# Whole tiles for VectorE's product and row sums, and half of one projection block in lanes 0 to 63

## The chip, the core and the metric

The kernel runs on one core of one Trainium2 chip. The metric is the device time of one launch in microseconds (us); 663.65 us is the median of three runs of the kernel before (663.64 to 663.78). A core has four compute engines here: TensorE (PE in the profile; PEld is its weight loads), VectorE (DVE), ScalarE (ACT) and GpSimd (POOL). SyncE (SP) issues nearly all transfers. Sixteen DMA engines move the data between device memory (HBM) and the on-chip memory SBUF, which has 128 partitions, called lanes below. TensorE writes its sums into PSUM.

## The reference

One decoding step of a transformer layer with two parallel branches, for a batch of four rows `x` of 640 numbers, in bf16:

```
xn  = layernorm(x)
q   = xn @ wq                                  # 32 heads of 128
s   = einsum('bhqd,bhkd->bhqk', q, k_cache) * 128 ** -0.5
o   = einsum('bhqk,bhkd->bhqd', softmax(s), v_cache)
A   = concat_heads(o) @ wo                     # 4096 x 640
B   = gated MLP of xn (gelu, layernorm, w_in, w_out)
out = x + A + B
```

The two caches hold 4 batches x 32 heads x 4096 positions x 128 numbers each. Every number of them is read once: 128 MB of keys and as much of values, out of 282 MB that the kernel moves. `wo` is 5 MB.

## The kernel before

**Tiles.** The 32 heads are worked through in 8 groups of 4 (`HG`, `HT`), and each group in 4 batch rows, which gives 32 turns, i = 4 * group + batch row. Turn i has one tile of keys and one of values, each 128 lanes x 16384 bf16 (4 MB): a lane holds 128 positions (`NC`) of one head, so that lanes 0 to 31 hold the first head of the group, and so on. Five SBUF slots (`KV_SLOTS`) take keys and values in rotation. `pump` (L140) issues the next loads of the list `loads` as soon as the tile five places earlier is marked as used; all of them go through the one queue of SP, in order. The keys of the last turns are loaded early (`EXTRA_K`), so that the last tile to arrive is one of values, cut in four (`V_CUTS`).

**A turn.** The order of instructions on PE, DVE, ACT and SP is written out by hand (L672 to L740). For the keys of turn i:

- `product` (L457, DVE) multiplies the tile in place by the query, one call for each half of the tile (`HC` = 64 positions).
- `fold_half` (L466, DVE) adds the upper 64 of 128 numbers onto the lower, a half tile a call.
- `sums` (L475, PE) adds eight slices of the folded half up in PSUM, with an identity as weights, into `s_ps`; 8 numbers are left for each position.
- `row_sums` (L486, DVE) adds those 8 up, a half a call.
- `lane_max` (L495, DVE), `lay_max` (L501, ACT), `spread_max` (L508, PE) and `head_max` (L515, DVE) find the largest score of a head; `exps` (L524, ACT) exponentiates, and L533 (POOL) lays the result out as `pm`, the weights for the values.

These last steps are done for turn i - 1 inside turn i. `blocks` (L548, PE, 32 matmuls) multiplies a tile of values by its `pm`; after each second tile ACT copies the result (L558), and `gather` (L569, PE) sorts it by head. In the turns before the end the values lag one turn behind the keys, later two and three. In the last turn the blocks of turns 28 and 29 are both done, and after the loop those of 30 and 31.

**A group's end.** `group_den` (POOL L593, PE L600, DVE L602) adds up the exponentials, `group_norm` (L607, DVE) divides, `group_turn` (L616, PE) and `group_pick` (L627, L635, DVE) move four rows of the projection's input into every lane, and `group_proj` (L647, PE) multiplies by the group's block of `wo` (128 lanes x 4 rows x 640, 640 KB, one transfer, L159). Only the last group's block is laid out by head and comes in four transfers (L157). The blocks of the groups 6 and 7 are issued behind the last values, and their projections are the last matmuls of the kernel; ACT and DVE then copy the sums (L737, L738), and two small transfers store them.

The order of one turn before:

```
product(i, 0); row_sums(i-1, 1); maxima of i-1; group_pick and group_proj of an earlier group
fold_half(i, 0); head_max(i-1); exps(i-1); sums(i, 0); product(i, 1)
blocks(j), group_den; row_sums(i, 0); fold_half(i, 1); gather(j), group_norm
sums(i, 1); group_turn; pump()
```

Of the kernel before, what the change touches and what calls it, by code (L numbers as in the profile page):

```python
# [9 lines left out]
FP32 = mybir.dt.float32  # L10
BF16 = mybir.dt.bfloat16
ACT = mybir.ActivationFunctionType
ALU = mybir.AluOpType
AX = mybir.AxisListType
# [7 lines left out]
def kernel(  # L22
# [14 lines left out]
    nc = tc.nc  # L37
    P = nc.NUM_PARTITIONS
    Bsz, Sq, D = A_x.shape
    _, H, S, Dh = A_k_cache.shape  # L40
# [4 lines left out]
    scale_qk = float(Dh) ** -0.5  # L45
# [3 lines left out]
    HT = 4  # L49
    HG = H // HT  # L50
    NT = HG * Bsz
    LN = P // HT
    NC = HT * S // P
    HC = NC // 2
    HD2 = Dh // 2
    RW = 8
# [4 lines left out]
    NOH = D // 2  # L61
# [8 lines left out]
    const = ctx.enter_context(tc.tile_pool(name="const", bufs=1))  # L70
    work = ctx.enter_context(tc.tile_pool(name="work", bufs=1))
    small = ctx.enter_context(tc.tile_pool(name="small", bufs=2))
    PSUM = bass.MemoryType.PSUM
    ps_s = ctx.enter_context(tc.tile_pool(name="ps_s", bufs=2, space=PSUM))
    ps_pv = ctx.enter_context(tc.tile_pool(name="ps_pv", bufs=2, space=PSUM))
    ps_m = ctx.enter_context(tc.tile_pool(name="ps_m", bufs=2, space=PSUM))
    ps_out = ctx.enter_context(tc.tile_pool(name="ps_out", bufs=1, space=PSUM))
# [12 lines left out]
    for c0, c1 in ((0, HT), (HT, DC)):  # L90
        t = slot("wq")[:, 0 : (c1 - c0) * HD].rearrange("p (c n) -> p c n", n=HD)
# [58 lines left out]
    wo_h = A_wo.rearrange("(j h p) n -> j p h n", p=P, h=HT)  # L150
    wo_tiles = {}

    def load_wo(j):
        wo_tiles[j] = wop.tile([P, HT, D], BF16, name="wo")
        if j == HG - 1:
            for hh in range(HT):
                nc.sync.dma_start(out=wo_tiles[j][:, hh, :], in_=wo_h[j][:, hh, :])  # L157
            return
        nc.sync.dma_start(out=wo_tiles[j][:].rearrange("p r n -> p (r n)"), in_=wo_r[j])  # L159

# [10 lines left out]
    eps_tile = const.tile([P, 1], FP32)  # L171
    nc.vector.memset(eps_tile[:], eps)
    head_scale = const.tile([P, P], FP32)
    nc.vector.memset(head_scale[:], 0.0)
    lane_diag = const.tile([P, LN], FP32)
    nc.vector.tensor_reduce(
        out=lane_diag[:],
# [1 line left out]
        axis=AX.X,  # L179
        op=ALU.add,  # L180
    )
    for hh in range(HT):
        ps = slice(hh * LN, (hh + 1) * LN)
        nc.vector.memset(head_scale[ps, ps], scale_qk)
    ones_sq = const.tile([P, P], FP32)
    nc.vector.memset(ones_sq[:], 1.0)

# [10 lines left out]
            op=ALU.add,  # L198
        )

    hmask = const.tile([P, HT], FP32)
    nc.vector.memset(hmask[:], 0.0)
    for hh in range(HT):
        nc.vector.memset(hmask[hh * LN : (hh + 1) * LN, hh : hh + 1], 1.0)
    spread = const.tile([P, HT, HT, LN], BF16)
    nc.vector.tensor_copy(
        out=spread[:],
# [2 lines left out]
        ),  # L210
    )


    q_lanes = const.tile([HT * Bsz, Bsz, P], BF16)
    nc.vector.tensor_copy(
# [84 lines left out]
    def out_sum(half):  # L300
        return out_ps[OG * half : OG * half + Bsz, :]
# [132 lines left out]
    def stage_q(hg):  # L434
        g, ps = hg % CG, slice(hg % CG * LN, (hg % CG + 1) * LN)
        qr_ps = ps_m.tile([HT * Bsz, Dh], FP32, tag="m", name="qr_ps")
        for hh in range(HT):
            nc.tensor.matmul(
                out=qr_ps[:],
                lhsT=place[ps, hh, :],  # L440
                rhs=q_sb[ps, hg // CG, hh * Dh : (hh + 1) * Dh],
                start=(hh == 0),
                stop=(hh == HT - 1),
            )
        q_rows = small.tile([HT * Bsz, Dh], BF16, name="q_rows")
        nc.scalar.copy(out=q_rows[:], in_=qr_ps[:])
        qb_ps = ps_m.tile([P, Bsz, Dh], FP32, tag="m", name="qbc_ps")
        for b in range(Bsz):
            nc.tensor.matmul(
                out=qb_ps[:, b, :], lhsT=q_lanes[:, b, :], rhs=q_rows[:], start=True, stop=True  # L450
            )
        qbcs[hg] = small.tile([P, Bsz, Dh], BF16, name="qbc")
        nc.scalar.copy(out=qbcs[hg][:], in_=qb_ps[:])

    def product(i, half):
        t = k_tiles[i][:, half * HC : (half + 1) * HC, :]
        nc.vector.tensor_tensor(  # L457
            out=t,
            in0=t,
            in1=qbcs[i // Bsz][:, i % Bsz, None, :].to_broadcast([P, HC, Dh]),  # L460
            op=ALU.mult,
        )

    def fold_half(i, half):
        t = k_tiles[i][:, half * HC : (half + 1) * HC, :]
        nc.vector.tensor_tensor(  # L466
            out=t[:, :, 0:HD2], in0=t[:, :, 0:HD2], in1=t[:, :, HD2:Dh], op=ALU.add
        )

    def sums(i, half):  # L470
        t = k_tiles[i][:, half * HC : (half + 1) * HC, :]
        s = sums_ps[i, half] = ps_s.tile([P, HC, RW], FP32, name="s_ps")
        n = HD2 // RW
        for g in range(n):
            nc.tensor.matmul(  # L475
                out=s[:],
                lhsT=ident[:],
                rhs=t[:, :, g * RW : (g + 1) * RW],
                start=(g == 0),
                stop=(g == n - 1),  # L480
            )

    def row_sums(i, half):
        if half == 0:
            scores[i] = small.tile([P, NC], FP32, name="s_sb")
        nc.vector.tensor_reduce(  # L486
            out=scores[i][:, half * HC : (half + 1) * HC],
            in_=sums_ps.pop((i, half))[:],
            axis=AX.X,
            op=ALU.add,  # L490
        )

    def lane_max(i):
# [67 lines left out]
    def gather(i, stop=True):  # L561
        if i % 2 == 0:
            return
        hg, b = divmod(i, Bsz)
        if b == 1:
            pvs[hg] = ps_pv.tile([P, HT, Bsz], FP32, tag="pv", name="pv")
        pv_sb = blocks_sb.pop(i)
        for k in range(GC):
            nc.tensor.matmul(  # L569
                out=pvs[hg][:, :, b - 1 : b + 1],  # L570
                lhsT=pv_sb[:, k * Dh : (k + 1) * Dh],
                rhs=sel[:, k, :, :],
                start=(k == 0),
                stop=stop and k == GC - 1,
            )
# [67 lines left out]
    def group_proj(hg):  # L643
        o_n = gr.pop(hg)
        for hh in range(HT):
            for half in range(2):
# [5 lines left out]
                    stop=(hg == HG - 1 and hh == HT - 1),  # L652
                )

    def group(i, fn):
        if 0 <= i < NT and i % Bsz == Bsz - 1:
            fn(i // Bsz)

    def at(i, fn, *args):
        if 0 <= i < NT:  # L660
            fn(i, *args)
# [10 lines left out]
    with tc.manual_schedule(engines={E.PE, E.DVE, E.Activation, E.SP}):  # L672
        stage_q(0)
        gmlp()
        used.update(occupants[:3])
        pump()
        for i in range(NT):
            j = turns.get(i)
            product(i, 0)
            at(i - 1, row_sums, 1)  # L680
            at(i - 1, lane_max)
            at(i - 1, lay_max)
            at(i - 1, spread_max)
            group(turns.get(i - 1, -1), group_pick)
            if turns.get(i - 1, -1) // Bsz < HG - 2:
                group(turns.get(i - 1, -1), group_proj)
            fold_half(i, 0)
            at(i - 1, head_max)
            at(i - 1, exps)
            sums(i, 0)  # L690
            product(i, 1)
            if i % Bsz == 2 and i // Bsz + 1 < HG:
                stage_q(i // Bsz + 1)
            due = [] if j is None else [j]
            if i == NT - 1:
                due += range(j + 1, NT - 2)
            for n, jj in enumerate(due):
                if n:
                    gather(due[n - 1])
                blocks(jj)  # L700
                group(jj, group_den)
                used.add(("v", jj))
            row_sums(i, 0)
            fold_half(i, 1)
            if due:
                gather(due[-1])
            for jj in due:
                group(jj, group_norm)
            sums(i, 1)
            for jj in due:  # L710
                group(jj, group_turn)
            used.add(("k", i))
            pump()
            if i % Bsz == 2 and i // Bsz < HG - 2:
                load_wo(i // Bsz)
        load_wo(HG - 2)
        load_wo(HG - 1)
        row_sums(NT - 1, 1)
        lane_max(NT - 1)
        lay_max(NT - 1)  # L720
        spread_max(NT - 1)
        head_max(NT - 1)
        exps(NT - 1)
        blocks(NT - 2)
        group_den(HG - 1)
        blocks(NT - 1, 0, V_CUTS[1])
        gather(NT - 1, stop=False)
        for c0, c1 in zip(V_CUTS[1:], V_CUTS[2:]):
            pairs(NT - 1, c0, c1)
        group_norm(HG - 1)  # L730
        group_proj(HG - 2)
        group_proj(HG - 1)

        res = work.tile([P, NOH], BF16, name="res")
        out_v = out.flatten_outer_dims()
        r0, r1 = slice(0, Bsz), slice(OG, OG + Bsz)
        nc.scalar.copy(out=res[r0], in_=out_ps[r0])  # L737
        nc.vector.tensor_copy(out=res[r1], in_=out_ps[r1])  # L738
        nc.scalar.dma_start(out=out_v[:, 0:NOH], in_=res[r0])
        nc.sync.dma_start(out=out_v[:, NOH:D], in_=res[r1])  # L740
# [30 lines left out]
```

## Time and profile before

| what | value |
|---|---|
| median of three runs | 663.65 us (663.64 to 663.78) |
| span of the profiled execution, first to last instruction | 661.6 us |
| what lies around the span (median less span) | 2.05 us |
| moved from and to HBM | 282.24 MB read, 0.01 MB written, 427 GB/s over the span |
| DVE busy | 491.5 us, 74% |
| PE busy | 348.7 us, 53%, at a mean granted clock of 0.726 |
| POOL busy | 151.3 us, 23% |
| ACT busy | 49.3 us, 7% |

The page gives no time for the profiled execution other than its span, so the sums below are made against the span. Each engine's share of busy time is a mean over the whole span. The row of DMA digits in the page's second part is the mean busy share of the sixteen DMA engines in each fortieth of the span. In the answers of the trace a line of the timeline has the start, the busy time, the engine, the kernel's line and the operation, and in brackets the idle time before it with what ended that. In a table by windows the columns are the busy time of each engine (with the number of instructions), the granted TensorE clock, the share of the DMA engines that was busy and GB/s.

### The profile page before, as it was taken

The page shows a single profiled execution, that of the slowest core. Times are in us where ns is not written, and L with a number is a line of the kernel's source. Part 1 is how long each engine was busy: PE and PEld are TensorE (multiplying, and loading weights), DVE is VectorE, ACT ScalarE, POOL GpSimd, SP SyncE. Part 2 cuts the span into 40 slices and gives each one's busy share as a digit, 9 for nine tenths or more (in the row PEclk, how much of TensorE's full clock was granted, in tenths as well). Part 3 has the DMA queues.
Part 4 walks back from the last instruction along what each step waited for, and adds up shares of the span by engine and source line. Part 5 has one row for each costly group of instructions (what it writes and reads, how often), then busy time and mean ns, then how long its engine had stood idle before and what let it go on. Part 6 is the DMA issues. An engine that isn't in the chain of part 4 may idle for free.

```text
span 661.6 us, 5115 instructions
## 1 busy us (share of the span) xinstructions
PE 348.7 (53%) x2109; PEld 144.6 (22%) x2109; DVE 491.5 (74%) x334; ACT 49.3 (7%) x138; POOL 151.3 (23%) x57
## 2 busy tenths in 40 slices
PE   2526653646445455663745654465643756435567
PEld 1402211212121121221212222121211312112124
DVE  2299797867789677788776698776787899777950
ACT  0201100001000010001000000000100000000010
POOL 3002222112222112222112222112222133122230
PEclk9999676776767777766678657777576577688585
DMA  9999999999999999999999999999999999999997
GB/s 368 432 438 429 430 440 427 440 423 434 442 416 447 424 433 442 423 440 424 433 440 423 440 428 431 442 421 442 422 435 442 422 441 428 427 442 428 429 428 289
DMA packets 11971, 282.57 MB, mean 427 GB/s; under 512 B 1344, under 2 KB 1964, under 8 KB 3244
## 3 DMA queue, kind: packets, MB, share of 16 engines
q1 hardware_dynamic: 11928, 282.25, 99.2%
q8 instruction: 16, 0.26, 0.1%
q14 instruction: 7, 0.06, 0.0%
q10 hardware_dynamic: 20, 0.01, 0.0%
HBM read 282.24 MB, written 0.01 MB: 427 GB/s over the span
## 4 chain that ended last, share of the span: by engine, by line
issue 49%; DMA 25%; POOL 15%; DVE 7%; PE 3%; SPq 1%; ACT 0%; POOLq 0%; DVEq 0%; ACTq 0%
DMA k_nat<-in_A_k_cache_dram 20%; POOL pm L533 15%; DMA wo<-in_A_wo_dram 4%; DVE k_nat L457 4%; DVE k_nat L466 2%; PE s_ps L475 2%; PE pv_acc L548 1%; SPq L123 0%; DVE s_sb L486 0%; PE out_ps L647 0%; PE pv L569 0%; POOL own_sum L593 0%; DVE m L495 0%; SPq L92 0%; SPq L104 0%
## 5 line engine op out<-in xcount | busy, mean ns | idle before, releaser
L457 DVE TENSOR_TENSOR k_nat<-k_nat,qbc 128x8192 bf16<-128x8192 bf16 x64 | 282.8, 4419 | 97.8 <-DMA k_nat<-in_A_k_cache_dram 97.8
L533 POOL TENSOR_TENSOR pm<-p,hmask_bf 128x512 bf16<-128x512 bf16 x32 | 142.5, 4452 | 490.9 <-ACT p L524 490.9
L475 PE MATMUL s_ps<-k_nat,ident 128*128 128x512 bf16 x512 | 189.2, 536 | 68.2 <-DVE k_nat L466 68.2
L466 DVE TENSOR_TENSOR k_nat<-k_nat 128x4096 bf16<-128x4096 bf16 x64 | 151.8, 2372 | 0.0
L548 PE MATMUL pv_acc<-v_nat,pm 128*32 128x512 bf16 x1008 | 88.6, 514 | 39.1 <-POOL pm L533 35.5
L508 PE MATMUL max_ps<-lay,head_scale 128*128 128x32 f32 x64 | 18.7, 383 | 171.4 <-ACT lay L501 171.4
L475 PEld LDWEIGHTS <-ident 128*128 128x128 bf16 x512 | 67.9, 135 | 171.1 <-issue 153.8
L508 PEld LDWEIGHTS max_ps<-lay,head_scale 128*128 128x128 f32 x64 | 14.6, 284 | 186.0 <-ACT lay L501 186.0
L548 PEld LDWEIGHTS <-pm 128*32 128x32 bf16 x1008 | 30.2, 120 | 96.2 <-POOL pm L533 52.0
L486 DVE TENSOR_REDUCE s_sb<-s_ps 128x64 f32<-128x512 f32 x64 | 43.3, 677 | 4.2 <-PE s_ps L475 4.2
L501 ACT ACTIVATE lay<-lane_diag,m 128x32 f32<-128x32 f32 x32 | 10.3, 321 | 395.9 <-DVE m L495 395.9
L602 DVE RECIPROCAL rden<-den 128x16 f32<-128x16 f32 x8 | 2.1, 257 | 32.2 <-PE den L600 32.2
L569 PE MATMUL pv<-sel,pv_sb 128*128 128x8 f32 x128 | 19.4, 279 | 9.3 <-ACT pv_sb L558 9.3
L569 PEld LDWEIGHTS pv<-sel,pv_sb 128*128 128x128 f32 x128 | 17.9, 217 | 17.2 <-ACT pv_sb L558 17.2
L524 ACT ACTIVATE p<-s_sb,nb 128x128 bf16<-128x128 f32 x32 | 12.9, 402 | 63.5 <-DVE nb L515 63.5
L558 ACT COPY pv_sb<-pv_acc 128x512 f32<-128x512 f32 x16 | 9.4, 585 | 91.8 <-PE pv_acc L548 91.8
L495 DVE TENSOR_REDUCE m<-s_sb 128x1 f32<-128x128 f32 x32 | 9.1, 286 | 1.1
L285 PE MATMUL q_ps<-wq,xnT 128*32 128x512 bf16 x40 | 4.5, 631 | 8.3 <-DMA wq<-in_A_wq_dram 8.3
L647 PE MATMUL out_ps<-wo,o_r 128*4 128x320 bf16 x56 | 8.0, 433 | 0.3 <-DMA wo<-in_A_wo_dram 0.3
L292 DVE CAST q_sb<-q_ps 128x512 bf16<-128x512 f32 x1 | 0.7, 691 | 9.3 <-PE q_ps L285 9.3
L515 DVE TENSOR_REDUCE nb<-max_ps 128x1 f32<-128x32 f32 x32 | 5.9, 183 | 0.9 <-PE max_ps L508 0.9
L607 DVE TENSOR_TENSOR o_n<-pv,rden 128x16 bf16<-128x16 f32 x8 | 1.3, 168 | 6.7 <-PE pv L581 6.7
(94 smaller groups left out, 91.4 us busy)
## 6 DMA issues: line engine op xcount, KB each, us to landing
k_nat<-in_A_k_cache_dram SPq DMA_DIRECT2D x32, 4096.0 KB, 37.9
v_nat<-in_A_v_cache_dram SPq DMA_DIRECT2D x31, 4096.0 KB, 33.6
wo<-in_A_wo_dram SPq DMA_DIRECT2D x7, 640.0 KB, 38.1
wq<-in_A_wq_dram SPq DMA_DIRECT2D x1, 4096.0 KB, 12.8
w_sb<-in_B_w_in_dram SPq DMA_DIRECT2D x1, 2160.0 KB, 19.5
v_nat<-in_A_v_cache_dram SPq DMA_DIRECT2D x1, 2048.0 KB, 24.5
wq<-in_A_wq_dram SPq DMA_DIRECT2D x1, 1024.0 KB, 14.8
v_nat<-in_A_v_cache_dram SPq DMA_DIRECT2D x1, 1024.0 KB
```

Of the source, the lines that this page charges most:

```text
L457: nc.vector.tensor_tensor(out=t, in0=t, in1=qbcs[i // Bsz][:, i % Bsz, None, :].to_broadcast([P, HC, Dh]), op=ALU.mult,)
L466: nc.vector.tensor_tensor(out=t[:, :, 0:HD2], in0=t[:, :, 0:HD2], in1=t[:, :, HD2:Dh], op=ALU.add)
L475: nc.tensor.matmul(out=s[:], lhsT=ident[:], rhs=t[:, :, g * RW : (g + 1) * RW], start=(g == 0), stop=(g == n - 1),)
L486: nc.vector.tensor_reduce(out=scores[i][:, half * HC : (half + 1) * HC], in_=sums_ps.pop((i, half))[:], axis=AX.X, op=ALU.add,)
L495: nc.vector.tensor_reduce(out=m1[:], in_=scores[i][:], axis=AX.X, op=ALU.max)
L501: nc.scalar.activation(out=d[:], in_=lane_diag[:], func=ACT.Copy, scale=maxes[i][:, 0:1])
L508: nc.tensor.matmul(out=ps[:], lhsT=head_scale[:], rhs=maxes[i][:], start=True, stop=True)
L524: nc.scalar.activation(out=p[:], in_=scores.pop(i)[:], func=ACT.Exp, bias=nb[:], scale=scale_qk, accum_out=acc[hg % NACC][:, b : b + 1],)
L533: nc.gpsimd.tensor_tensor(out=p_m[b][:, :, e : e + GC * HT].rearrange("p g (c h) -> p g c h", h=HT), in0=p[:].rearrange("p (g c) -> p g c" ...
L548: nc.tensor.matmul(out=pv_acc[g * LN : (g + 1) * LN, :], lhsT=pm[:, c // GC, :], rhs=v_nat[:, c : c + GC, :].rearrange("p c d -> p (c d)") ...
L558: nc.scalar.copy(out=pv_sb[:], in_=pv_acc[:])
L569: nc.tensor.matmul(out=pvs[hg][:, :, b - 1 : b + 1], lhsT=pv_sb[:, k * Dh : (k + 1) * Dh], rhs=sel[:, k, :, :], start=(k == 0), stop=stop ...
```

## The change

Two things are changed, and the order of a turn with them.

1. `product` and `row_sums` are one call a tile in place of two. `fold_half` and `sums` stay halves. `s_ps` now holds a whole tile's sums (two PSUM banks), with one buffer in place of two. The order of a turn becomes `product(i)`, `row_sums(i-1)`, the maxima, `group_den`, `group_norm` and `group_turn` of an earlier group, `fold_half(i, 0)`, `head_max` and `exps` of i - 1, `sums(i, 0)`, `group_pick`, `fold_half(i, 1)`, `sums(i, 1)`, `group_proj`, and only then `blocks(j)` and `gather(j)`. So the values' matmuls move behind the second half's sums, and `group_den`, `group_norm` and `group_turn` move from the turn of the group's last values into the turn after it.
2. The block of `wo` of group 3 (`MIX`) is split. Its first 256 rows are spread over all 128 lanes, two rows (2560 bytes) a lane. Its other 256 rows go to lanes 0 to 63 alone, four rows (5120 bytes) a lane, into a tile `wo_low`, in eight transfers of 8 lanes (40 KB) that lie four lanes apart, one at the end of each of the turns 7 to 14. `mix_turn`, `mix_pick` and `mix_proj` take the place of the group functions for group 3: 6 matmuls in place of 4, four DVE operations in place of two, and 12 projection matmuls in place of 8.

Some constants in the start-up are built by reductions in place of memsets.

```diff
-    ps_s = ctx.enter_context(tc.tile_pool(name="ps_s", bufs=2, space=PSUM))
+    ps_s = ctx.enter_context(tc.tile_pool(name="ps_s", bufs=1, space=PSUM))
...
+    MIX = 3
+    LOW = P // 2
+    ME, MJ = 8, 4
+    wo_low = const.tile([P, HT, D], BF16, name="wo_low")
+    wo_pairs = A_wo[MIX * HT * P : (MIX * HT + 2) * P].rearrange("(p r) n -> p (r n)", r=2)
+    wo_quads = A_wo[(MIX * HT + 2) * P : (MIX + 1) * HT * P].rearrange(
+        "(g e j r) n -> g j e (r n)", e=ME, j=MJ, r=HT
+    )
+
+    def load_low(n):
+        g, j = divmod(n, MJ)
+        lanes = slice(g * ME * MJ + j, (g + 1) * ME * MJ, MJ)
+        nc.sync.dma_start(
+            out=wo_low[lanes].rearrange("p r n -> p (r n)"), in_=wo_quads[g, j]
+        )
...
+        if j == MIX:
+            nc.sync.dma_start(
+                out=wo_tiles[j][:, 0:2, :].rearrange("p r n -> p (r n)"), in_=wo_pairs
+            )
+            return
...
-    def product(i, half):
-        t = k_tiles[i][:, half * HC : (half + 1) * HC, :]
+    def product(i):
+        t = k_tiles[i]
...
     def sums(i, half):
-        t = k_tiles[i][:, half * HC : (half + 1) * HC, :]
-        s = sums_ps[i, half] = ps_s.tile([P, HC, RW], FP32, name="s_ps")
+        if half == 0:
+            sums_ps[i] = ps_s.tile([P, NC, RW], FP32, name="s_ps")
+        c = slice(half * HC, (half + 1) * HC)
...
-    def row_sums(i, half):
-        if half == 0:
-            scores[i] = small.tile([P, NC], FP32, name="s_sb")
+    def row_sums(i):
+        scores[i] = small.tile([P, NC], FP32, name="s_sb")
         nc.vector.tensor_reduce(
-            out=scores[i][:, half * HC : (half + 1) * HC],
-            in_=sums_ps.pop((i, half))[:],
-            axis=AX.X,
-            op=ALU.add,
+            out=scores[i][:], in_=sums_ps.pop(i)[:], axis=AX.X, op=ALU.add
         )
...
+    def mix_proj(hg):
+        two, four = gr.pop(hg)
+        parts = [(two, r, wo_tiles[hg], P) for r in range(2)]
+        parts += [(four, r, wo_low, LOW) for r in range(HT)]
...
+    mixed = {group_turn: mix_turn, group_pick: mix_pick, group_proj: mix_proj}
...
-            product(i, 0)
-            at(i - 1, row_sums, 1)
+            before = turns.get(i - 1, -1)
+            product(i)
+            at(i - 1, row_sums)
             at(i - 1, lane_max)
             at(i - 1, lay_max)
             at(i - 1, spread_max)
-            group(turns.get(i - 1, -1), group_pick)
-            if turns.get(i - 1, -1) // Bsz < HG - 2:
-                group(turns.get(i - 1, -1), group_proj)
+            group(before, group_den)
+            group(before, group_norm)
+            group(before, group_turn)
             fold_half(i, 0)
             at(i - 1, head_max)
             at(i - 1, exps)
             sums(i, 0)
-            product(i, 1)
+            group(before, group_pick)
+            fold_half(i, 1)
+            sums(i, 1)
...
-            for n, jj in enumerate(due):
-                if n:
-                    gather(due[n - 1])
+            for jj in due:
                 blocks(jj)
-                group(jj, group_den)
                 used.add(("v", jj))
-            row_sums(i, 0)
-            fold_half(i, 1)
-            if due:
-                gather(due[-1])
-            for jj in due:
-                group(jj, group_norm)
-            sums(i, 1)
-            for jj in due:
-                group(jj, group_turn)
+                gather(jj)
             used.add(("k", i))
             pump()
             if i % Bsz == 2 and i // Bsz < HG - 2:
                 load_wo(i // Bsz)
+            if 0 <= MIX * Bsz + 2 - i < 2 * MJ:
+                load_low(MIX * Bsz + 2 - i)
```

## The prediction, as it was made before the result was known

> **What bounds the kernel now.** I read the page's second and third parts first, then the costliest groups, the timeline and windows of the last 30 us, and last the trace's single DMA packets.
>
> ```profile
> span 661.6 us, 5115 instructions
> ...
> DVE  2299797867789677788776698776787899777950
> ...
> DMA  9999999999999999999999999999999999999997
> ...
> q1 hardware_dynamic: 11928, 282.25, 99.2%
> q8 instruction: 16, 0.26, 0.1%
> q14 instruction: 7, 0.06, 0.0%
> ...
> L457 DVE TENSOR_TENSOR k_nat<-k_nat,qbc 128x8192 bf16<-128x8192 bf16 x64 | 282.8, 4419 | 97.8 <-DMA k_nat<-in_A_k_cache_dram 97.8
> ...
> L486 DVE TENSOR_REDUCE s_sb<-s_ps 128x64 f32<-128x512 f32 x64 | 43.3, 677 | 4.2 <-PE s_ps L475 4.2
> ...
> v_nat<-in_A_v_cache_dram SPq DMA_DIRECT2D x31, 4096.0 KB, 33.6
> ```
>
> The sixteen DMA engines are busy from the first fortieth to the last, 99.2% in the one load queue. DVE waits for keys (97.8 us). A load lands 33.6 us after its issue and a tile takes 9.7 us of the stream, so issues run some 24 us ahead. In the middle only what the DMA engines carry counts.
>
> In the packets sixteen streams can be followed, since each packet starts 3 to 4 ns before its predecessor on the same engine ends: a 32 KB packet takes 1.210 us from start to start, a 5120-byte one 0.193. The streams end far apart: the last part of the last `wo` block lands from 655.46 to 658.27 us. They drift apart at instruction fetches (q8, q14). A 16 KB fetch sets its stream back 1.42 us (itself 0.88 to 1.01, the next packet 1.7 in place of 1.21). The sixteen of them go round eight streams, two each. An 8 KB fetch costs 0.53 to 0.96 us and falls on others; three fall on one stream, at DVE's 51st, 188th and 323rd instruction record. Against an untouched stream the eight are 2.38 to 2.67 us late at the end, DVE's 2.10, the rest at most 0.6. The four-lane load of `x` at the start ran on streams of this early half (three of the four can be matched).
>
> ```profile
> 635.60 1.91 PE L548 MATMUL pv_acc<-v_nat,pm 128*32 128x512 bf16 x32 [0.53 <-DMA v_nat<-in_A_v_cache_dram]
> ...
> 639.17 1.89 PE L475 MATMUL s_ps<-k_nat,ident 128*128 128x512 bf16 x8
> ...
> 645.28 3.60 PE L548 MATMUL pv_acc<-v_nat,pm 128*32 128x512 bf16 x32 [2.30 <-DMA v_nat<-in_A_v_cache_dram]
> ...
> 650.15 1.90 PE L548 MATMUL pv_acc<-v_nat,pm 128*32 128x512 bf16 x16 [0.72 <-DMA v_nat<-in_A_v_cache_dram]
> ...
> 656.64 1.23 PE L647 MATMUL out_ps<-wo,o_r 128*4 128x320 bf16 x8 [0.28 <-DMA wo<-in_A_wo_dram]
> ```
>
> At the end PE waits for each tile of values and then for `wo`: the end hangs on the slowest stream too, with PE only 0.3 to 0.7 us ahead of it. Its clock matters:
>
> ```profile
> 633.40:643.60 10.20, 6.80 (x82) 3.52 (x75) 4.69 (x6) 1.20 (x3) 1.37 (x1) 1.00 1.00 432
> 643.60:650.00 6.40, 4.14 (x34) 1.81 (x34) 0.26 (x1) 0.20 (x2) 1.21 (x2) 0.50 0.96 406
> ```
>
> The sixth figure after the length is the clock: full, then half, and 32 matmuls of `blocks` take 1.91 or 3.60 us with it.
>
> **The change, part by part.** The sum is made against the 661.6 us span; the median stands 2.05 us above it, and that part (launch, outside the span) is kept.
>
> *Whole product and row sums.* From L457 (4.419 us for 8192 elements) and an undisturbed fold (2.28 for 4096) an element costs 0.52 ns and an instruction 0.14 us: 8.7 us for the whole tile against 8.84. Row sums: 0.677 for 512 elements and `lane_max` 0.286 for 128 give about 1.2 against 1.35. DVE saves 0.3 us a turn, some 10 in all, beside the stream: worth nothing, since a turn is 19.4 us and DVE's work about 15.
>
> *Later releases.* Keys are freed when the second half's sums end: 8.7 + 1.2 + 0.3 + 2.3 + 0.1 + 2.4 = 15 us after landing plus 1.9 to 3.6 of sums, about where they were. Values are freed behind that, 4 to 7 us later than the 15 to 16.6 us of before. SP's queue behind them moves as much, out of 24 us of lead: nothing. Were that lead gone, each turn would pay it: 32 x 4 us.
>
> *The block of group 3.* On every stream eight packets of 2560 bytes take the place of eight of 5120: -8 x 0.193 + 8 x 0.098 (half, by size) = -0.76 us. The eight small transfers add one 5120-byte packet and a 4-byte one (0.006) each to whichever eight streams take them: +8 x 0.199 = +1.59, net +0.83. That they are the early eight is not shown; if so, the late eight end at 2.67 - 0.76 = 1.91 and no other at more than DVE's. If they were the late eight, the end moves by +0.08. The four-lane load speaks for the first, and I take it. [...]
>
> *What a small transfer costs besides.* The four parts of the last `wo` block (160 KB, 10 KB a stream) land 0.41 us apart, and their bytes alone take 0.38: 0.03 each, 0.3 for eight. Far end: the first packets of the kernel, on empty streams, took about 1.9 us in place of 1.21: 0.7 each, 5.6 for eight. The streams are never empty here, so I take the near end. [...] SP issues each in 0.33 to 0.43 us, behind the loads of its turn.
>
> *Fetches.* DVE's list shrinks from 328 to 266 rows, its records from 384 to some 322. Its third fetch came at record 323, so it falls away or comes too late to matter: -0.84 on DVE's stream, which then ends at 2.10 - 0.84 + 0.83 = 2.09. That is now the latest. Were it kept: 2.93, the end +0.26. PE's list grows by 12 rows and its last fetch was at 649.0: sixteen as before.
>
> So the last landing moves by 2.09 - 2.67 = -0.58 us, to 657.7.
>
> *The end on PE.* The keys of turn 30 land at 606.5. DVE then: product to 615.2, row sums 616.4, `lane_max` 616.7. The end of group 6 has moved here (before, in the turn ahead, beside idle time): ACT 0.32, PE 0.64, `den` 0.4 to 0.6, reciprocal 0.26, `o_n` 0.17, so DVE folds from 618.7; with a wait for `o_ps` and the pick (1.0) the second fold ends at 624.4, where 621.9 stood before. Turn 31: product 633.0, sums and maximum 634.5, folds 636.7 and 639.1. PE sums from 636.7: at half clock 3.57 us, then the second half at once. This is unbroken work; before, a full clock came at 633.4 after a 3.4 us piece busy throughout. So it rises between 640.2 and 643.6, and the sums end at 642.2 to 643.9. Now come both `blocks`, formerly done by 637.5: to 646.1 (647.8); ACT's copy and `gather` 1.8: 647.9 (649.6); behind them the last `spread_max` 648.3 (650.0); `blocks(30)` to 650.3 (652.0), meanwhile maximum, exponentials, POOL's 1.04 and 0.22, `den`: 651.1 (652.8). So the last tile's first part starts 1 to 2.7 us later than 650.15. At full clock it, copy, `gather` and pairs end near 655.5 (657.3). `wo` of group 6 lands at 656.0, and the eight projection pairs at 0.13 us (0.267 at half) reach the last part by 657.0 (658.3), against its landing at 657.7. Cover: 0.7 us in the good phase, none in the other (+0.6). At full clock the last pair starts and ends some 0.3 us sooner. I put the end on PE at 0.
>
> Sum: 661.6 - 0.6 = 661.0, and 663.05 by the median.
>
> **The rivals.**
> 1. *The balance buys nothing* (small transfers on the wrong streams, DVE's third fetch kept, or PE 0.6 late): +0.3 to 0, 663.6 to 663.9. For it: three separate small terms of the size of the gain.
> 2. *PE's tail becomes the bound: slower.* If the clock stays at half, `blocks` take 3.6 us each: sums end 643.9, `blocks` 651.1, `gather` 653.7, maximum 654.4, `blocks(30)` 658.0, the last tile from 658.7, where 650.15 stood; the end +8 us, 671. A drop to half in the middle gives +2 to 4, 665.5 to 667.5. It decides once the last tile starts later than about 653.5. For it: 643.6 to the end ran at half. Against: that drop followed a 3.4 us piece with PE 37% busy, and the new order leaves no such gap. [...]
> 3. *The small transfers or POOL hold the stream: slower.* 5.6 us by the far end above, 669. POOL's `pm` takes 4.56 us beside DVE and 1.04 alone, so a whole product may hold it 4.3 us longer, out of the 24 us lead.
> 4. *Faster by more.* All of -0.76 on the late streams, 0.3 on PE and the 0.2 us by which the last pair began after its data give 1.26: 662.4; past 0.2% it takes something that the profile does not show: 662.2.
>
> **How the numbers follow.** 0.2% is 1.33 us, about what a measurement of this kernel tells from no change. Forecast -0.6: 0.45; rival 1: 0.18; rival 2: 0.17; rival 3: 0.07; rival 4: 0.13. Same: 0.45 + 0.18 = 0.63; slower 0.24; faster 0.13. The likeliest's own range is 662.5 to 663.6. The range goes from 662.3 (some 0.07 below) to 666.3, into the middle of rival 2 (some 0.12 above).
>
> **What will show it.** Right: DMA digits of 9 throughout; the last part of the last `wo` block landing near 657.7, over 2.1 us or less; two fetches on DVE's stream; `wo_low` issues that land like their neighbours; L548's last tile starting at 651 to 653 at full clock, and PE's last wait again on `wo`. Wrong: a half clock between 643 and 655 with PE unbroken up to the last matmul, idle DMA slices, or a later stream among those with the small packets.

## The result: one microsecond slower

The changed kernel took 664.71 us in the median of 21 executions, the kernel before 663.65 us in the median of 21 beside it: +1.06 us, 0.16%. The ratio of the two, over all of these, is 1.0024 with an interval of 1.0015 to 1.0033. Some executions of most kernels here took about 5 us or more longer (two of the 21 of the changed one, which lift that ratio; in the two that were profiled, of runs 3 and 5, 388 GB/s were moved from 34 to 69 us in place of 433), so medians are compared below. The spans of all executions are on record too: their median is 662.9 us for the changed kernel and 661.8 or 661.9 us for the kernel before beside the runs below. The profiled execution of before, with 661.6 us, was a quick one, so what is read from the two profiles against each other comes out some 0.2 us too large. The forecast was 663.05 us. The time lies in the range that was given (662.3 to 666.3), but on the other side of the kernel before.

### The profile after

The page of the changed kernel: the span, VectorE's and the DMA engines' rows of forty slices, the load and instruction queues, the sums of all DMA engines' shares, then the two groups that the first part of the change remade.

```profile
span 662.9 us, 5094 instructions
...
DVE  3299788677787766788777788776778699767970
...
DMA  9999999999999999999999999999999999999996
...
q1 hardware_dynamic: 12056, 282.25, 99.0%
q8 instruction: 16, 0.26, 0.1%
q14 instruction: 6, 0.05, 0.0%
...
L498 DVE TENSOR_TENSOR k_nat<-k_nat,qbc 128x16384 bf16<-128x16384 bf16 x32 | 280.7, 8771 | 122.2 <-DMA k_nat<-in_A_k_cache_dram 98.0
...
L527 DVE TENSOR_REDUCE s_sb<-s_ps 128x128 f32<-128x1024 f32 x32 | 39.0, 1217 | 3.3 <-PE s_ps L517 3.3
```

The DMA engines are still busy throughout, and VectorE still waits 98.0 us for keys (97.8 before). A whole product takes 8.77 us, whole row sums 1.22. The end, by TensorE's timeline (start, length, instructions, and in brackets what it waited for):

```profile
651.41 1.05 PE L586 MATMUL pv_acc<-v_nat,pm 128*32 128x512 bf16 x16
653.20 1.06 PE L607 MATMUL pv<-sel,pv_sb 128*128 128x8 f32 x8 [0.75 <-ACT pv_sb L596]
...
656.13 0.59 PE L619 MATMUL pv<-pm,v_nat 128*128 128x4 bf16 x16 [0.67 <-DMA v_nat<-in_A_v_cache_dram]
657.66 1.23 PE L685 MATMUL out_ps<-wo,o_r 128*4 128x320 bf16 x8 [0.94 <-DMA wo<-in_A_wo_dram]
658.68 1.28 PE L685 MATMUL out_ps<-wo,o_n 128*4 128x320 bf16 x8
```

The last line of before, to set beside this:

```profile
657.66 1.28 PE L647 MATMUL out_ps<-wo,o_n 128*4 128x320 bf16 x8
```

TensorE now has its work done early and waits 0.94 us for `wo`, where it had waited 0.28; the last projections start at 658.68 instead of 657.66. That is +1.02 us. In the windows of the tail (length, TensorE's busy time, granted clock, DMA share, GB/s) the clock is lower in the first (0.60, before 1.00) and full in the second, where it had dropped to half:

```profile
633.40:643.60 10.20, 6.36 (x26) 0.60 0.98 424
643.60:650.00 6.40, 5.65 (x98) 1.00 0.95 406
```

So the loss is in the streams of the DMA engines. Their single packets show it. Below is, for the last whole tile but one (around 632 us), when each of the sixteen streams ended its part, in ns after the first one:

```
before   0  121  157  252  442  753  757 1136 2257 2537 2586 2657 2790 2807 2828 2832
after    0  556 1315 1319 1420 1571 1999 2375 2409 2524 2596 2655 2697 2751 4050 4335
```

The last part of the last `wo` block lands at 659.29 us, 1.02 later than the 658.27 of before. Fourteen streams are done with it by 657.7, just as forecast. Two stand apart, 1.3 and 1.6 us behind the rest in the row above. The trace tells which they are: the ones that served TensorE's fifth and sixth instruction fetch (at 197.3 and 238.1 us) and its 13th and 14th (534.1, 571.9). The first packets of a small transfer follow a stream's part of a tile within 5 to 6 ns (at 219 us), so that the streams that take it (the takers) can be named, by their offset in ns:

```
after, tile at 209.6:    0  266  299  355  367  432  447  538  861  923 1093 1492 1527 1577 1772 1814
small transfer, 219.3:   0  266  356  367  447  861  923 1577
```

1577 is the stream of the fifth fetch, moved there by it from 156; 447 is that of the sixth. Both take a packet of 0.199 us from every one of the eight small transfers, and have two fetches of 1.42 us each as well. These terms add up to where the two end: 1577 + 8 x 199 + 1420 = 4589 and 447 + 8 x 199 + 2 x 1420 = 4879. Of the streams that neither take nor serve a fetch of TensorE's, the earliest stands at 538 ns in that row and at 0 around 632 us, which leaves 4051 and 4341 against the 4050 and 4335 seen.

The rest of the span's +1.3 us lies behind the last matmul: 2.97 us to the end of the span in place of 2.68. VectorE's last instruction but one, a drain, starts at 662.58 us, 0.38 us after SyncE's (662.20), and all wait for it in the final barrier; in the kernel before it starts 0.03 us after SyncE's (661.20 and 661.17).

### The profile page after: what moved, and what is told of

The parts are those of the page before. It is cut to its first block, busy times and chain, and to the rows that moved or that the text cites. A ratio compares the mean times of both kernels' runs of the same rounds, so it can differ in the third digit from the quotient of the medians.

```text
span 662.9 us, 5094 instructions
## 1 busy us (share of the span) xinstructions
PE 310.8 (47%) x2115; PEld 142.0 (21%) x2115; DVE 487.0 (73%) x266; ACT 49.2 (7%) x138; POOL 86.8 (13%) x57
## 4 chain that ended last, share of the span: by engine, by line
DMA 59%; DVE 15%; PE 13%; issue 12%; SPq 1%; ACT 0%; DVEq 0%; ACTq 0%
DMA k_nat<-in_A_k_cache_dram 55%; PE s_ps L517 9%; DVE k_nat L498 6%; DVE k_nat L507 6%; DMA wo<-in_A_wo_dram 4%; PE pv_acc L586 3%; DVE s_sb L527 2%; DVE m L533 1%; PE out_ps L685 0%; PE max_ps L546 0%; SPq L123 0%; SPq L103 0%; PE den L638 0%; ACT lay L539 0%; SPq L92 0%
## 5 line engine op out<-in xcount | busy, mean ns | idle before, releaser
L498 DVE TENSOR_TENSOR k_nat<-k_nat,qbc 128x16384 bf16<-128x16384 bf16 x32 | 280.7, 8771 | 122.2 <-DMA k_nat<-in_A_k_cache_dram 98.0
L517 PE MATMUL s_ps<-k_nat,ident 128*128 128x512 bf16 x512 | 185.5, 542 | 51.6 <-DVE k_nat L507 51.6
L571 POOL TENSOR_TENSOR pm<-p,hmask_bf 128x512 bf16<-128x512 bf16 x32 | 79.7, 2491 | 560.7 <-ACT p L562 560.7
L507 DVE TENSOR_TENSOR k_nat<-k_nat 128x4096 bf16<-128x4096 bf16 x64 | 146.0, 2282 | 0.0
L517 PEld LDWEIGHTS <-ident 128*128 128x128 bf16 x512 | 64.6, 132 | 161.2 <-issue 103.2
L586 PE MATMUL pv_acc<-v_nat,pm 128*32 128x512 bf16 x1008 | 61.6, 380 | 0.0
L527 DVE TENSOR_REDUCE s_sb<-s_ps 128x128 f32<-128x1024 f32 x32 | 39.0, 1217 | 3.3 <-PE s_ps L517 3.3
L586 PEld LDWEIGHTS <-pm 128*32 128x32 bf16 x1008 | 25.9, 96 | 28.5 <-issue 7.5
L607 PE MATMUL pv<-sel,pv_sb 128*128 128x8 f32 x128 | 16.9, 259 | 11.8 <-ACT pv_sb L596 11.8
L562 ACT ACTIVATION_READ_ACCUMULATOR p<-s_sb,nb 128x1 f32 x32 | 6.0, 187 | 0.0
```

Source lines behind the costliest of these rows:

```text
L498: nc.vector.tensor_tensor(out=t, in0=t, in1=qbcs[i // Bsz][:, i % Bsz, None, :].to_broadcast([P, NC, Dh]), op=ALU.mult,)
L507: nc.vector.tensor_tensor(out=t[:, :, 0:HD2], in0=t[:, :, 0:HD2], in1=t[:, :, HD2:Dh], op=ALU.add)
L517: nc.tensor.matmul(out=sums_ps[i][:, c, :], lhsT=ident[:], rhs=k_tiles[i][:, c, g * RW : (g + 1) * RW], start=(g == 0), stop=(g == n - 1),)
L527: nc.vector.tensor_reduce(out=scores[i][:], in_=sums_ps.pop(i)[:], axis=AX.X, op=ALU.add)
L562: nc.scalar.activation(out=p[:], in_=scores.pop(i)[:], func=ACT.Exp, bias=nb[:], scale=scale_qk, accum_out=acc[hg % NACC][:, b : b + 1],)
L571: nc.gpsimd.tensor_tensor(out=p_m[b][:, :, e : e + GC * HT].rearrange("p g (c h) -> p g c h", h=HT), in0=p[:].rearrange("p (g c) -> p g c" ...
```

## The experiments

Theory S: two of the eight streams that take the small transfers also carry fetches, and end last. Its rivals: T, the new order of the turn costs the microsecond; L, each small transfer costs something whichever streams carry it. Each diff is against the kernel that is named; the spare loads of runs 5, 6, 9, 11 and 12 read 80 to 160 KB of `wo` more, which nothing uses.

### Each part alone

Run 1 is the changed kernel without the second part.

```diff
-        if j == MIX:
-            nc.sync.dma_start(out=wo_tiles[j][:, 0:2, :]..., in_=wo_pairs)
-            return
...
-            if 0 <= MIX * Bsz + 2 - i < 2 * MJ:
-                load_low(MIX * Bsz + 2 - i)
```

> The whole product, the whole row sums and the new order of the turn, with the block of group 3 loaded as before (no small transfers, no half loads). Theory S (the microsecond comes from two of the streams that carry TensorE's instruction fetches and also take the small packets; about 0.3 us more from VectorE's last fetch, which falls on the final barrier): the last part of wo lands at about 658.3 us in the profile, as before, and the time is 663.65 us, or 663.95 if VectorE's last fetch lies at the end. Theory T (the new order and its longer tail on TensorE cost the microsecond): 664.7 us, as with the whole change. If executions some 5 us longer come from the new order and not from the small transfers, some of them are seen here as well.

Measured: 663.63 us in the median of 12, the kernel before 663.59 beside it, ratio 1.0004 (0.9992 to 1.0016). Run 2 is the kernel before with the second part alone (and `group_pick` moved ahead of `spread_max`).

```diff
+        if j == MIX:
+            nc.sync.dma_start(out=wo_tiles[j][:, 0:2, :]..., in_=wo_pairs)
+            return
...
+            if 0 <= MIX * Bsz + 2 - i < 2 * MJ:
+                load_low(MIX * Bsz + 2 - i)
```

> The kernel before with the second part of the change alone: group 3's block in one half-size transfer and eight transfers of eight lanes; the product and the row sums stay in halves. S: two streams end about 0.8 to 1.0 us after the latest of before (near 659.1 to 659.3 us in the profile), and the time is 664.5 to 664.7 us. T: 663.65 us or less, since the tail on TensorE is that of before.

Measured: 664.25 us (11), ratio 1.0009 (1.0000 to 1.0018). TensorE's last two steps, first of run 1, then of run 2:

```profile
656.89 1.23 PE L649 MATMUL out_ps<-wo,o_r 128*4 128x320 bf16 x8 [0.95 <-DMA wo<-in_A_wo_dram]
657.91 1.28 PE L649 MATMUL out_ps<-wo,o_n 128*4 128x320 bf16 x8
```

```profile
657.83 1.23 PE L683 MATMUL out_ps<-wo,o_r 128*4 128x320 bf16 x8 [0.95 <-DMA wo<-in_A_wo_dram]
658.85 1.28 PE L683 MATMUL out_ps<-wo,o_n 128*4 128x320 bf16 x8
```

T falls: the new order alone costs nothing that these medians show (the last part lands at 658.52 us in its profile, whose span is 661.9). The second part alone costs 0.66 us, a little less than S had said, and its last stream ends at 659.46 us in the profiled execution (664.60 us long). There three stand apart (3990, 4344 and 4732 ns, the next 2913): the last two are those of the fifth and sixth fetch, the first is VectorE's, which kept its three fetches.

### Other ways to load the 64 lanes

Run 3 is the changed kernel with one load of all 64 lanes.

```diff
-    wo_quads = A_wo[...].rearrange("(g e j r) n -> g j e (r n)", e=ME, j=MJ, r=HT)
+    wo_all = A_wo[...].rearrange("(p r) n -> p (r n)", r=HT)
...
-        nc.sync.dma_start(out=wo_low[lanes]..., in_=wo_quads[g, j])
+        nc.sync.dma_start(out=wo_low[:LOW]..., in_=wo_all)
...
-            if 0 <= MIX * Bsz + 2 - i < 2 * MJ:
-                load_low(MIX * Bsz + 2 - i)
+            if i == MIX * Bsz - 2:
+                load_low(0)
```

> The changed kernel with the 64 lanes of group 3's block in one transfer of 64 lanes in place of eight of eight lanes: the same bytes, the same layout up to the order of the lanes, spread over all sixteen streams (four packets of 5120 bytes on each). S: every stream carries the bytes of before, the latest ends near 658.3 us, and the time is 663.65 us plus up to 0.3 for VectorE's fetch at the end, so 663.7 to 664.0. T: 664.7 us, as the order of the turn is that of the changed kernel. L (each small transfer costs something fixed, whichever streams carry it): about 663.7 as well, so this run parts S and L from T only.

Measured: 665.59 us (12). Every theory is wrong here. The windows around that load (length, then busy time of TensorE, its weight loads, VectorE, ScalarE and GpSimd, clock, DMA share, GB/s), of the changed kernel and of run 3:

```profile
277.00:289.00 12.00, 4.28 (x47) 2.15 (x45) 8.70 (x2) 0.58 (x1) 0.00 (x0) 0.76 1.00 428
```

```profile
277.00:289.00 12.00, 8.42 (x56) 3.66 (x56) 7.19 (x4) 1.08 (x3) 2.60 (x2) 0.78 1.00 362
```

The DMA engines are busy all the time (share 1.00) and move 15% less. By the packets, a tile with a `wo` block and this load should take 9.68 + 1.55 + 4 x 0.193 + 0.01 = 12.01 us on a stream and took 13.76: 1.75 us lost on all sixteen, with 23 packets of 32 KB at up to 2.3 us in place of 1.21. That is about the whole excess of the run (665.6 - 663.6 = 2.0).

Run 4 is the changed kernel with eleven transfers of six neighbouring lanes, in the turns 4 to 14.

```diff
+    LL = 6
...
+        lanes = slice(n * LL, min((n + 1) * LL, LOW))
+        nc.sync.dma_start(out=wo_low[lanes]..., in_=wo_all[lanes])
```

> The changed kernel with the 64 lanes of group 3's block in eleven transfers of six neighbouring lanes (the last has four) in place of eight of eight. S, if the two doubly loaded streams are the last two of the eight that take the small packets: no stream with a TensorE fetch takes one, so those eight end some 0.76 us earlier than before (about 657.5 to 657.7); the six takers end at most at 2.1 + 11 x 0.199 - 0.76 = 3.5 us after an untouched stream's old end if one of them has VectorE's fetches too, where the latest of before stood at 2.67, and VectorE's third fetch (0.84 of that) lies late: 2.7; so the last landing is within 0.1 of before, and the time is 663.6 to 664.0 us. L: eleven small transfers cost more than eight, so 665.0 us or more. T: 664.7 us.

Measured: 666.57 us (5). Here too 32 KB packets are stretched, 1.25 to 1.6 us long, around nearly every one of the small transfers. A measure of it is what all 32 KB packets took above 1.214 us, over sixteen: 1.53 us in the changed kernel (the start and the fetches), 2.69 in run 4. S can't be judged with that in the way. I thought of the neighbouring lanes, several streams writing into the same few. Run 7 is run 4 with the lanes of a transfer spread out:

```diff
-        lanes = slice(n * LL, min((n + 1) * LL, LOW))
+        lanes = slice(n, LL * LS, LS) if n < LS else slice(LL * LS, LOW)   # LL, LS = 6, 10
```

> The changed kernel with the 64 lanes in ten transfers of six lanes ten apart and one of four neighbouring lanes: the number of transfers of the run with six neighbouring lanes, which stretched the 32 KB packets of the other streams, but with the lanes of a transfer spread out. Theory N (packets of several streams into neighbouring lanes hold up the stream that also writes there; spread lanes do not): no stretched packets around the small transfers, and then S holds: the eight with TensorE's fetches end 0.76 us earlier than before, the last of the takers within 0.1 of the latest of before, and the time is 663.6 to 664.0 us. If six-lane transfers stretch the others wherever their lanes lie: 666 us or more, as with neighbouring lanes. If the number of small transfers is what costs: above the 664.7 us of the changed kernel.

Measured: 666.59 us (8), 3.17 us of stretching. Theory N falls: lanes far apart stretch as much. But eight lanes four apart don't, in the changed kernel, nor did the loads of the next runs.

### Spare loads: how many lanes, and which

These runs are the kernel before with four more small loads.

```diff
+    SPARE, STEP = 8, 4
+    spare = const.tile([P, HT * D], BF16, name="spare")
+    def load_spare(n):
+        lanes = slice(n, n + SPARE * STEP, STEP)
+        nc.sync.dma_start(out=spare[lanes], in_=wo_r[0][lanes])
...
+            if 7 <= i < 11:
+                load_spare(i - 7)
```

> The kernel before with four more transfers of eight lanes, four lanes apart, in turns 7 to 10 (40 KB each, 160 KB in all, read from wo into a tile that nothing uses). S (the eight streams that take an eight-lane transfer include two of the eight that carry TensorE's fetches): four times 0.199 us on eight streams, so two streams stand apart at the end, some 0.8 us behind the other six that carry fetches, and the time is 664.2 to 664.5 us. If no stream with a fetch takes them, as the prediction had it: only VectorE's stream becomes later, 2.10 + 0.80 = 2.9 against 2.67, so at most 663.85 us.

> The same with four transfers of six lanes, four lanes apart (30 KB each, 120 KB). S: the two streams with a fetch are the last two of the eight takers, so none of the six takers carries one; VectorE's stream ends at 2.10 + 0.80 = 2.9 against 2.67, the time is 663.6 to 663.85 us, and no two streams stand apart. L (what a small transfer costs does not depend on the stream): as the run with eight lanes.

> The kernel before with four spare transfers of four lanes, four lanes apart, in turns 7 to 10 (20 KB each, 80 KB). With six lanes one stream with a TensorE fetch was still among the takers (the third fetch's) and the time was 664.37 us. [...] If it is not: at most VectorE's stream is later, 2.26 + 0.80 = 3.06 against 2.83, so 663.6 to 663.9 us.

> The run with four spare transfers of eight lanes four apart once more, beside the run with neighbouring lanes: 664.3 to 664.8 us, and no stretched packets around the transfers.

Run 12 is run 5 again, run 9 has `SPARE = 4`, and this is run 6 against run 5:

```diff
-    SPARE, STEP = 8, 4
+    SPARE, STEP = 6, 4
```

Eight lanes took 664.68 us (12), a little more than S had said, and in run 12 664.40 (11), six 664.37 (11), four 664.22 (11), where 663.6 to 663.9 was expected (for four lanes 664.3 to 664.5 if a taker has a fetch of TensorE's). Before stood at 663.6 beside each. They stretch no packets: 1.56, 1.49 and 1.41 us by the measure above in runs 6, 9 and 12. In these kernels the final barrier is 0.25 us longer than before's 2.68, as SyncE waits first for the last store and has four more waits of 0.06 us behind that; the expectations had not counted this, and it is the larger part of what run 9 lies above its range. The last landing of `wo` tells the streams' part:

```
                     last landing   against 658.27   streams with a fetch among the takers
run 12, eight lanes      659.12          +0.85        two (fetches 5 and 6)
run 6, six lanes         658.96          +0.69        one (fetch 3)
run 9, four lanes        658.59          +0.32        none; VectorE's stream is last, 43 ns behind a fetch's
```

S holds, but not as I had put it for six lanes: one of the two streams takes six-lane transfers as well (offset 1543, moved there from 120 by the third fetch), so that run took +0.8 us and not the +0.2 expected. VectorE's stream, which is a taker too, ends only 27 ns ahead of it in that run (3613 and 3640 ns around 632 us), so run 6 by itself does not tell the two apart. In run 12 it does not matter: the two with fetches end at 3442 and 3588 ns, VectorE's at 3175. With four lanes no taker has a fetch of TensorE's. The round of fetches starts at another place in another program. Two streams that follow each other in it have the shortest fetches, 0.88 us against 0.92 to 1.1. In the changed kernel and runs 2, 8 and 12 these are the two takers (fetches 5 and 6), in run 6 they are fetches 3 and 4, of which the third's takes; by that sign alone they are 5 and 6 in runs 5 and 10, 3 and 4 in runs 9 and 11.

Run 11 goes after the stretching. Against run 12 it changes the lanes alone, and with them the rows of `wo` that are read:

```diff
-    SPARE, STEP = 8, 4
+    SPARE = 8
...
-        lanes = slice(n, n + SPARE * STEP, STEP)
-        nc.sync.dma_start(out=spare[lanes], in_=wo_r[0][lanes])
+        nc.sync.dma_start(out=spare[n * SPARE : (n + 1) * SPARE], in_=wo_r[0][n * SPARE : (n + 1) * SPARE])
```

> The kernel before with four spare transfers of eight neighbouring lanes (0 to 7, 8 to 15, 16 to 23, 24 to 31) in turns 7 to 10: the same bytes, turns and number as with eight lanes four apart, and nothing else changed. [...]

Measured: 665.77 us (7) against 664.40 for run 12 on the same chip, +1.37. The 32 KB packets of over 1.23 us around the four transfers, and how far these are above 1.213 in sum:

```
            run 11, neighbouring          run 12, four apart
219 us       8 packets, 1.20 us            none
239 us      29 packets, 3.48 us            none
258 us      34 packets, 5.01 us            none
280 us      25 packets, 2.83 us            none
```

The bytes, the turns and the number of the transfers are those of run 12, so it is the lanes. My estimate, from the stretching in run 4, had been 1 to 3 us at each transfer and 664.8 to 665.5 us; it is somewhat more. Lanes four apart cost nothing beyond their bytes (each taker 0.199 us). Neighbouring ones hold up streams that have no part in the transfer: the 29 packets at 239 us start within 2.1 us, in which eight takers start 16 at most. That the rows read are neighbours too is not needed for it, since run 7, with rows ten apart, stretches as well. Why neighbouring lanes and lanes ten apart stretch these packets and lanes four apart do not is not shown: no row of a trace names an engine or the lanes that it writes.

### VectorE's last instruction

Run 8 is the changed kernel with five instructions of the set-up moved from VectorE to GpSimd.

```diff
-    nc.vector.memset(ones_row[:], 1.0)
+    nc.gpsimd.memset(ones_row[:], 1.0)
...
-    nc.vector.tensor_copy(out=spread2[:], ...)
+    nc.gpsimd.tensor_copy(out=spread2[:], ...)
```

> The changed kernel with five of VectorE's instructions of the set-up (three fills, two copies) given to GpSimd, so that VectorE's list is five shorter and its last fetch may not come at all. If that fetch costs 0.3 us at the final barrier: from the last matmul to the end of the span 2.7 us in place of 2.97, and 664.4 us; the two late streams stay. If it costs nothing: 664.7 us.

Measured: 664.60 us (11), and from the last matmul to the end 2.69 us, as before. So the late instruction is gone with another end of VectorE's list (321 records in the changed kernel, 316 here). The median fell by 0.1 only, not by 0.3; the lowest times fell from 664.55 to 664.25. The median span did fall by 0.3 us, from 662.9 to 662.6, but what an execution takes beyond its span grew from 1.81 us to 2.00 in the median. The two late streams are there (4428 and 4472 ns, the next 3282).

### The streams spared

Run 10 gives the takers' part to four streams that carry no fetch of TensorE's: it is run 8 with head 3 alone in small transfers.

```diff
+                out=wo_tiles[j][:, 0:3, :], in_=wo_h[j][:, 0:3, :]
...
+        lanes = slice(32 * g + j, 32 * g + 16, 4)
+        nc.sync.dma_start(out=wo_low[lanes]..., in_=wo_quads[g, j])
...
+        parts = [(o_n[:, h, :], wo_tiles[hg][:, h, :]) for h in range(3)]
+        parts += [(o_r4[:, r, :], wo_low[:, r, :]) for r in range(HT)]
```

> The changed kernel with five instructions of the set-up on GpSimd, and with another share of group 3's block in small transfers: heads 0 to 2 over all 128 lanes, projected without a turn, and head 3 alone (160 KB) in eight transfers of four lanes four apart (lanes 0 to 15 and 32 to 47; lanes 16 to 31 hold zeros). Every stream loses 8 x 0.193 - 24 x 0.0475 = 0.40 us, the four takers get 8 x 0.199 = 1.59. If no stream with a TensorE fetch is among the lowest four: those end at 2.83 - 0.40 = 2.43, VectorE's (two fetches in place of three) at 2.26 - 0.84 + 1.19 = 2.61, so the last landing 0.2 us before that of the kernel before, and 663.2 to 663.6 us: the change as it was meant. If one is: 2.83 + 1.19 = 4.02, 1.2 us later, 664.8 us.

Measured: 663.75 us (11), 0.14 above the kernel before (ratio 1.0015, 0.9991 to 1.0038) and 0.85 below run 8, with as many small transfers, each of half the bytes. That rules L out. The "lowest four" of the expectation are the four takers; no run shows an order of the engines. TensorE's last steps of run 10, and the streams of run 8 and run 10 around 632 us:

```profile
656.62 1.23 PE L677 MATMUL out_ps<-wo,o_r 128*4 128x320 bf16 x8 [0.97 <-DMA wo<-in_A_wo_dram]
657.64 1.28 PE L677 MATMUL out_ps<-wo,o_n 128*4 128x320 bf16 x8
```

```
run 8    0  998 1494 1873 1909 1991 2176 2563 2847 2881 2952 3134 3173 3282 4428 4472
run 10   0  453  706 1119 1742 1794 2057 2600 2865 2885 2892 2921 3055 3092 3172 3299
```

No stream stands apart. The last one is now VectorE's (3299), the last landing 658.23, against 658.27 in the quick execution of before that was profiled. The spans show the 0.2 us that I had worked out: 661.6 us in the median against 661.8. But the executions of run 10 take 2.14 us beyond their span in the median, those of before 1.78, and that eats the gain. Runs 8 and 10, with five instructions of the set-up moved to GpSimd, are those with the most of it; what it is was not looked into. No version here beats the kernel before in time.

## Why the prediction was wrong

**What bounds the kernel:** right. The load streams set the time (the load queue at 99.0%), and only the last one counts (659.29 us, where fourteen are done by 657.7).

**Whole product and row sums, later releases, GpSimd:** right. 8.77 and 1.22 us for 8.7 and 1.2, VectorE's busy time down from 491.5 to 487.0 us, and run 1 shows them worth nothing, with the values' later release hidden.

**The end on TensorE:** right. The last tile's first part started at 651.41 (651.1 to 652.8 expected), the clock was full from 643.6 to 650 (it rose at 641.6, within the 640.2 to 643.6 that the prediction took from one rise of before), and the cover, 0.94 us, was of the size given (0.7). Rival 2 did not come.

**The block of group 3:** wrong, and this is the step that failed: "*That they are the early eight is not shown; if so, the late eight end at 2.67 - 0.76 = 1.91 and no other at more than DVE's. [...] The four-lane load speaks for the first, and I take it.*" Fourteen streams did what it says. But the takers and the streams with fetches overlap in two. The four-lane load was sound evidence, for four lanes: run 9 shows that the takers of four lanes carry no fetch of TensorE's, and run 12 that those of eight lanes include two that do. It could not speak for streams that it did not use. The other branch of that step had a slip besides: "*If they were the late eight, the end moves by +0.08.*" By its own terms it moves by -0.76 + 1.59 = +0.83 us, of which nothing is taken off, since such a stream was the last already. With the right sum, an overlap of even one stream would have been seen to turn the sign. The traces show +1.02, +1.19 (run 2) and +0.68 (run 8), as the streams' starts differ.

**What a small transfer costs besides:** right for these lanes. In every tile with a small transfer the takers fall back by 0.199 us and the others by nothing; the far end, 5.6 us, did not come near. It is right only because of the lanes: run 11 pays 1.37 us more than run 12 for four transfers to neighbouring lanes.

**Fetches:** half right. VectorE's third fetch no longer falls into the stream (an 8 KB fetch stands at 663.41 us, behind the span). But VectorE's last instruction but one now comes late, and the final barrier with it by 0.3 us, which had no term in the sum; run 8 shows it gone with a shorter list.

**The 2.05 us around the span:** too large by a quarter of a microsecond. It sets the median time against the span of another execution. Taken execution by execution it is 1.79 us for the kernel before and 1.81 for the changed one, and the forecast span of 661.0 us would have stood for 662.8. This has no part in the sign.

Rival 1 named the mechanism, "small transfers on the wrong streams", but priced it, with the slip, at 663.9 at most.

## What to carry to other kernels

In this kernel, whose load streams are busy from end to end (99.0%), a transfer over few lanes was not spread: it was paid in full by a few streams (0.199 us by each of eight for eight lanes, the same ones each time), and the kernel ended with the slowest stream (+1.02 us), so ask of each stream, not of the mean, what else it carries. Instruction fetches were such a load (1.42 us each, two to a stream), and the streams that serve them have to be read from the packets of the trace; evidence from four of the streams said nothing of the next four (run 9 against run 12). If few lanes must be loaded, try which: four apart was free here beyond the bytes (no stretched packet, run 12), neighbouring lanes (1.20 to 5.01 us of stretching in sum at a transfer, run 11) and lanes ten apart (3.17 us over sixteen against 1.53 in the changed kernel, run 7) were not.

## What the runs showed that I had not expected

- Lanes decide: eight lanes four apart cost 0.199 us on each of eight streams and nothing elsewhere; eight neighbouring ones stretch the 32 KB packets by 1.2 to 5.0 us in sum at each transfer, and 64 lanes in one load cost 1.75 us on all sixteen.
- TensorE's sixteen instruction fetches go round eight streams, of which two take eight-lane transfers and none takes four-lane ones, and the round starts elsewhere from program to program. No wait of TensorE in these profiles is put down to one; but each takes 1.42 us from a load stream, and on the last stream that is the kernel's time (the two late ones of the changed kernel carry two each and end 1.3 and 1.6 us behind the rest).
- A list of 321 records on VectorE ended with a drain 0.38 us behind SyncE's at the final barrier. Those of 316 (run 8), 319 (runs 4 and 7), 320 (run 1) and 324 (run 3) did not, with 0.03 us each, so it is not the length by itself. Why was not settled.
